# The last two blocks cut as 704 and 256 tokens, the last stores on two queues, the first batch's scaling on two engines, and a new order of all steps

## The chip, the cores and the metric

One core of one Trainium2 chip runs the whole kernel. The metric is the device time of one execution in microseconds (us), the median over several runs. The core's engines are TensorE (PE, with its weight loads listed apart as PEld), VectorE (DVE), ScalarE (ACT), GpSimd (POOL) and SyncE (SP). DMAs are issued from the instruction streams of SP, ACT and POOL.

## The reference

Inputs and output are fp32; q, k and v have 4 batches of 6080 tokens and 256 columns.

```python
qn = q / (np.linalg.norm(q, axis=1, keepdims=True) + 1e-06)   # norms over the 6080 tokens
kn = k / (np.linalg.norm(k, axis=1, keepdims=True) + 1e-06)
s = kn.transpose(0, 2, 1) @ qn / tau                           # 256 x 256 for each batch
a = softmax(s)                                                 # over the last axis
x = (v @ a).reshape(24320, 256)
h = x @ w_in                                                   # 256 -> 2048
out = gelu_tanh(h) @ w_out                                     # 2048 -> 256
```

## The kernel before, in words

**Folding.** For each batch the kernel computes the 256 x 256 matrix of scores and multiplies its exponentials into w_in: `aw` is 256 x 2048, with the softmax's row factors `rs` applied when it is copied out of PSUM. So a token goes from v through `aw`, Gelu and w_out, and v @ a is never formed. All matmuls take bf16 operands and add up in fp32.

**Blocks.** The tokens are cut into 25 blocks, m = 0 to 24, by `SIZES` (L44): five of 1024 and one of 960 in a batch, but in the last batch five of 1024, one of 512 and one of 448. A block is two halves of `hc` tokens (512, 480, and 256 and 224 for the last two), and `hc` is the number of columns that most of its matmuls stream. For each half v is transposed into `vT`: mostly by a cast into a bf16 buffer in DRAM (steps `lv`) and a transposing DMA (`lt`), and for block 0 and the first half of block 1 by PE (`pe_vt`, L341, from what `load_v0` has loaded).

**First layer.** Its 16 chunks of 128 columns of `aw` are done in one of two ways. Plain chunks: steps `jXt` (`mm1_one`, L559) are two matmuls for chunk X and half t, or for both halves at once when t = 2 and the block is narrow; `JXt` (`gelu_one`, L574) is their Gelu on ACT. Pairs of chunks: steps `spm1` to `spm7` (`small`, from L626) take seven matmuls instead of eight for two chunks and both halves, in the manner of Strassen's product, with sums of weights (`sums_w`) and of vT (`sums_v`, steps `vs`); `cq`, `y5`, `ap`, `ax` and the four Gelus `G0, G1, Gr, Gx` (`set_step`) put them together on ACT and DVE.

**Second layer.** Seven products `M1` to `M7` for a block (`product`, L735), each eight matmuls of `hc` columns in two parts A and B, on sums that DVE makes (`T1` to `T4`, `sums_g`). `x1`, `y5`, `y6`, `ap`, `ax`, `a12` combine them, `c11` to `c22` transpose 32 x 32 pieces into the output tile `ot` (pool `yout` with three buffers), and `O0` and `O1` (`store`, L783) write each half with four DMAs of 32 partitions.

**Order.** Nothing is scheduled by a planner at run time. The stretch up to the first `aw` is written out in the code; from there on the text `ORDER` (from L983, 4067 steps) lists every step of all blocks and of batches 1 to 3, and the engines receive their instructions in the order of that list. PSUM's eight banks are handed out by `take` and `give` from a first-in, first-out list (L77), so a new order also changes which step inherits whose bank. The tile framework adds the semaphore waits.

**The head, batch 0.** q and k come in six chunks of rows; for each, ACT and DVE square the elements, PE adds up the squares (`ss_rows`, L213) and the product G of q and k (`gram_first`, L199). The last chunk comes in five pieces (`PIECES`, L137) and is squared by rows (`square_rows`, L174). After it PE transposes v of block 0 (`pe_vt`), `scores` (L359) makes the exponentials on ACT and DVE, DVE and ACT copy one half each of `vT` out of PSUM (L348 to L354), ACT loads the Gelu table (L903), and `first_aw` (L379) computes the sums, the row factors and the first 512 columns of `aw`: DVE scales columns 0 to 255 in four steps (L403), ACT columns 256 to 511 in two (L406). `ORDER` begins with block 0's chunks 0, 1, 2 (`j00`, `j10`, `j20`) and the next part of `aw` (`aw2`, L512, scaled at L525).

**The last stores.** In `store`, the last block's first half to be stored goes to SP, POOL, ACT, POOL, the second alternately to ACT and SP; of the block before it, the third and fourth DMA go to POOL; all others go to SP. A DMA that SP or ACT issues reports to one of eight semaphores, which are used in turn; POOL's DMAs have eight of their own.

Of the kernel before, what the change touches and what calls it, by code (L numbers as in the profile page):

```python
# [18 lines left out]
def kernel(  # L19
# [24 lines left out]
    SIZES = [[1024] * 5 + [960]] * (B - 1) + [[1024] * 5 + [512, 448]]  # L44
# [295 lines left out]

    def pe_vt(m, t):  # L341
        VPS[m, t] = ps = take(("vps", m, t), 1, [128, 2, HALF], f"vt_ps{m}_{t}", BF16)[0]
        for s in range(HALF // 128):
            for cc in range(2):
                nc.tensor.transpose(ps[:, cc, s * 128 : s * 128 + 128],
                                    V0[m, t][:, s, cc * 128 : cc * 128 + 128], ident_bf)

    def pe_vt_copy(m, t, cc):  # L348
        if (m, t, cc) == (0, 0, 1):
            nc.scalar.copy(vt(m)[:, t, cc, :], VPS[m, t][:, cc, :])  # L350
        else:
            nc.vector.tensor_copy(vt(m)[:, t, cc, :], VPS[m, t][:, cc, :])
        if cc == 1:
            give(("vps", m, t))  # L354
# [24 lines left out]
    def first_aw():  # L379
# [21 lines left out]
        for u in range(2):  # L401
            for ic in range(2):
                nc.vector.tensor_scalar_mul(AW[b][:, ic, u * 128 : u * 128 + 128],  # L403
                                            ps[0][ic][:, u * 128 : u * 128 + 128], rs[:, ic : ic + 1])
        for ic in range(2):
            nc.scalar.activation(AW[b][:, ic, 256:512], ps[1][ic], AF.Copy, scale=rs[:, ic : ic + 1])  # L406
# [346 lines left out]
    XS, CS, OT, LAST_OUT = {}, {}, {}, []  # L753
# [28 lines left out]
    def store(m, tj):  # L782
# [13 lines left out]
        if m == LAST:  # L796
            LAST_OUT.append(tj)
# [27 lines left out]
    with tc.manual_schedule():  # L825
# [49 lines left out]
        square_rows(c, 1, 0, 5, "dve")  # L875
# [3 lines left out]
        ss_rows(c, 1, range(0, 5))  # L879
# [19 lines left out]
        pe_vt(0, 0)  # L899
        scores()  # L900
        pe_vt_copy(0, 0, 0)
        pe_vt_copy(0, 0, 1)
        nc.scalar.preload_act_table(AF.Gelu_apprx_tanh)  # L903
# [94 lines left out]
1:s5Gx b1:r3.3 1:s6m3 1:s7y5 0:c21 1:s5m4 1:s6m7 1:M1A 1:s7cq 1:s7m6 1:s5Gr b1:f2.1 1:M1B 1:T3a
1:s6ax 1:s6m4 1:s7m2 b1:r4.0 1:s6G1 b1:r4.1 1:s7ap 1:s7m3 1:T1a 1:s7m7 b1:zq3 1:s6Gx 1:x1 b1:lk6
1:s6Gr b1:lq6 1:s7ax 2:j30 1:s7G0 b1:lq7 b1:r4.2 1:s7G1 2:j11 1:s7m4 2:j01 1:T2a 1:s7Gx 1:s7Gr  # L1000
b1:f3.1 2:j20 2:vs0 2:vs1 1:M2A 2:J30 2:J20 1:T3b 2:s2m1 3:lv1 1:M2B 2:J11 2:s2m5 1:c11 2:s2cq 1:M6A
1:T1b b1:zq5 2:s2m6 1:M5A 2:s2m2 2:s2y5 b1:zq4 2:s2ap 1:T2b 2:s2G0 2:J01 2:j10 b1:dk4 1:M5B 2:vs2
0:c22 2:j21 2:s3m1 2:J10 2:s2m3 1:y5 0:O1 2:J21 3:lt1 2:s2G1 1:M6B 2:s3cq 2:j00 2:J00 1:ap 2:s2m7
# [6 lines left out]
b1:r5.3 2:s6ap 2:s7m5 2:s5Gr 2:s6m7 b1:f5.2 b1:lk7 2:T3a 2:s6ax 2:s7cq 2:s6m3 b1:lk8 2:M1B 2:s7m6  # L1010
3:j30 2:s6m4 2:s7y5 b1:r6.0 2:s7m2 b1:lq8 4:lv1 2:s7ap 2:s7m3 2:s7m7 2:s6G1 2:s6Gx 2:T1a 2:s6Gr
2:s7ax 2:T2a b1:r6.1 b1:r6.2 3:j00 b1:r6.3 3:J30 b1:lq11 b1:lk9 2:s7G0 2:s7G1 3:s2m1 3:J00 2:s7m4
b1:lq9 b1:f6.1 2:M5A 3:j11 2:s7Gx 3:j20 2:T3b 2:s7Gr 2:x1 3:j21 3:vs0 3:J11 b1:zq7 2:M2A b1:lk10
3:J21 3:j01 b1:f5.3 2:M2B 2:T1b 3:J20 3:J01 3:s2m5 3:vs1 5:lv1 3:s2cq b1:r7.0 2:c11 2:M6A b1:r7.1
3:s3m1 3:s2m6 2:M5B 3:s2m2 b1:r7.2 2:T2b 3:s2y5 b1:zk7 b1:r7.3 3:s2ap 3:s2m7 b1:lk11 3:vs2 b1:f5.4
3:s3cq b1:zq8 b1:dk8 3:s2ax 3:s2m3 b1:r8.0 2:y5 3:s2G1 5:lv0 3:s3m2 2:M6B 3:s3m5 3:s2m4 3:s3m6
3:s2G0 3:s3G0 3:j10 3:s3y5 b1:f7.1 3:s2Gr 3:s4m1 3:s2Gx b1:lq10 3:s4cq 2:ap b1:r8.1 2:M3A 3:s3ap
3:J10 3:s3m3 2:T4a 3:s3G1 3:s3m7 2:M3B 3:s4m5 b1:r8.2 3:s4m2 3:s3ax b1:f7.2 3:s5m1 b1:zq9 b1:zk9
2:M7A 3:s3m4 2:M7B 3:s4m6 3:s4G0 2:T4b 3:s4y5 3:s5m5 4:lt0 b1:r8.3 2:c12 3:s5cq 3:s3Gr b1:r9.0
b1:f9.1 b1:f7.3 3:s5m6 3:s6m1 3:s4ap 3:s5y5 2:ax 3:s4m3 3:s3Gx 3:s4G1 3:s4m7 3:s5ap 3:s5m2 3:s5G0  # L1020
2:M4A 3:s6cq 3:s4ax 3:s5m3 b1:r9.1 b1:f7.4 3:s6m5 1:O0 b1:dk10 3:s5m7 3:s4Gx 3:s6y5 3:s4m4 3:s4Gr
3:s6m6 3:s5G1 4:lt1 3:s6m2 2:M4B 3:s7m5 b1:r9.2 3:s5ax 3:s6ap 3:s6m7 3:s7m1 3:s5Gx 2:c21 3:s6m3
3:s5m4 3:s6G0 3:s6ax b1:r9.3 b1:r10.0 2:O0 b1:r10.1 3:s6m4 5:lt0 3:s7y5 3:s7cq b1:f8.1 b1:r10.2
b1:r10.3 3:s6Gx 3:s6Gr b1:r11.0 3:T3a 3:s7m6 b1:r11.1 4:j00 b1:r11.2 3:s5Gr 3:s6G1 3:s7ap 4:s2m1
b1:r11.3 4:J00 3:s7m3 3:s7m7 b1:gc 3:T1a 3:s7ax 3:M1A 3:T2a 4:s2cq 4:j11 4:s2m2 3:s7G1 3:s7m4 4:s3m1
4:vs0 3:s7Gx 4:s2G0 3:s7m2 5:lt1 4:J11 3:T3b 3:M1B 4:vs1 4:s2m5 3:M5A 3:T1b 3:s7Gr 3:x1 3:s7G0 3:M2A
# [288 lines left out]
```

## Time and profile before

| what | value |
|---|---|
| median of 3 runs | 683.74 us (683.71 to 683.79) |
| the profiled execution | 683.82 us |
| its span, first to last instruction | 682.1 us |
| granted PE clock, mean | 0.998 |
| PE busy | 660.3 us, 97%, 3412 matmuls |
| ACT busy | 640.7 us, 94%, 1241 instructions |
| DVE busy | 630.5 us, 92%, 935 instructions |
| POOL busy | 90.1 us, 13% |
| DMA | 78.80 MB, mean 116 GB/s |

Times inside the trace count from the start of the span. A busy share is an average over stages: PE is idle for a good part of the first 50 us, and hardly ever behind them. A line of the trace's timeline has the start and the busy time of a group of instructions, engine, line, operation, the tiles it writes and reads with their shapes, and in brackets the idle time ahead of it with what ended it. In the table of busy time by stretch the columns are the stretch, its length, busy time (and count) of PE, PEld, DVE, ACT and POOL, then the granted PE clock, the DMA engines' share and GB/s.

### The profile page before, as it was taken

To read this page: it belongs to the slowest core of one execution; us is meant where nothing else is said; L and a number is where in the kernel's file an instruction comes from. 1 tells how busy PE (TensorE), PEld (TensorE's weight loads), DVE (VectorE), ACT (ScalarE), POOL (GpSimd) and SP (SyncE) were. 2 spreads that over 40 slices of the span, in tenths; PEclk is the share of its full clock that TensorE was granted. 3 is DMA by queue.
4 is the path that set the end of the run, shared out by engine and by line. 5 is a ranking of instruction groups with operands and counts; after the bars stand their busy time and mean duration, and the time that the engine had idled before them with its cause. 6 is when DMAs were issued, how large, how long until landed. Compare 5 with 4: busy or idle time off the path is not lost.

```text
span 682.1 us, 10254 instructions
## 1 busy us (share of the span) xinstructions
PE 660.3 (97%) x3412; PEld 333.9 (49%) x3472; DVE 630.5 (92%) x935; ACT 640.7 (94%) x1241; POOL 90.1 (13%) x165
## 2 busy tenths in 40 slices
PE   3999999999999999999999999999999999999996
PEld 2844444544445454454444544454444444444465
DVE  3579999999999999999999999999999999999996
ACT  5389999999999999999999999999999999999983
POOL 4323112111100122101020201200000000000002
PEclk9999999999999999999999999999999999999999
DMA  9997868878545896646884477668343446262453
GB/s 241 208 254 134 148 116 140 144 124 147 109 81 105 130 170 112 116 91 116 137 142 78 82 133 137 100 117 132 61 80 62 78 68 118 43 86 46 76 100 60
DMA packets 164678, 78.80 MB, mean 116 GB/s; under 512 B 148545, under 2 KB 153025, under 8 KB 163905
## 3 DMA queue, kind: packets, MB, share of 16 engines
q0 software_dynamic: 18064, 39.84, 32.9%
q1 hardware_dynamic: 145552, 37.09, 30.3%
q10 hardware_dynamic: 1008, 1.22, 0.6%
q8 instruction: 27, 0.44, 0.3%
q14 instruction: 27, 0.21, 0.1%
HBM read 78.91 MB, written 36.57 MB: 169 GB/s over the span
## 4 chain that ended last, share of the span: by engine, by line
PE 79%; ACT 14%; DMA 4%; issue 2%; POOL 0%; DVE 0%; POOLq 0%; DVEq 0%; ACTq 0%
PE u L750 20%; PE rb L639 15%; PE j L571 11%; PE p L750 10%; PE qb L639 7%; PE c L750 5%; PE G L304 4%; DMA qk<-in_k_dram 4%; PE qa L639 3%; ACT qa L654 2%; ACT g L583 2%; PE awp L512 2%; ACT g L664 2%; ACT yw L657 2%; ACT g L673 2%
## 5 line engine op out<-in xcount | busy, mean ns | idle before, releaser
L750 PEld LDWEIGHTS <-wcomb 128*128 128x128 bf16 x1400 | 136.9, 98 | 143.4
L750 PE MATMUL u<-t,wcomb 128*128 128x512 bf16 (+3 forms) x590 | 144.1, 368 | 0.4
L583 ACT ACTIVATE g<-j 128x512 bf16<-128x512 f32 (+1 forms) x196 | 119.0, 664 | 2.0 <-PE j L571 2.0
L571 PE MATMUL j<-vT,aw 128*128 128x512 bf16 (+2 forms) x410 | 114.6, 376 | 1.0 <-ACT aw L406 0.3
L659 DVE TENSOR_TENSOR qb<-rb,yw 128x512 f32<-128x512 f32 (+3 forms) x142 | 95.7, 676 | 9.2 <-PE rb L639 4.1
L639 PE MATMUL rb<-tv,sw 128*128 128x512 bf16 (+3 forms) x276 | 99.8, 372 | 0.4
L662 DVE TENSOR_TENSOR xw<-rb,yw 128x512 f32<-128x512 f32 (+3 forms) x142 | 94.5, 667 | 6.1 <-PE rb L639 3.1
L750 PE MATMUL p<-g,wcomb 128*128 128x512 bf16 (+3 forms) x393 | 96.4, 368 | 0.4
L673 ACT ACTIVATE g<-xw 128x512 bf16<-128x512 f32 (+3 forms) x142 | 94.3, 666 | 0.0
L670 ACT ACTIVATE g<-rb 128x512 bf16<-128x512 f32 (+3 forms) x142 | 88.7, 636 | 2.6 <-PE rb L639 2.5
L654 ACT ACTIVATE qa<-rb 128x512 f32<-128x512 f32 (+3 forms) x142 | 89.3, 633 | 1.4 <-PE rb L639 0.5
L667 ACT ACTIVATE g<-qb 128x512 bf16<-128x512 f32 (+3 forms) x142 | 88.7, 630 | 1.9 <-PE qb L639 1.5
L657 ACT ACTIVATE yw<-qb 128x512 f32<-128x512 f32 (+3 forms) x142 | 89.1, 632 | 1.5 <-PE qb L639 1.0
L664 ACT ACTIVATE g<-qa 128x512 bf16<-128x512 f32 (+3 forms) x142 | 88.7, 631 | 0.3 <-PE qa L639 0.2
L639 PEld LDWEIGHTS <-sw 128*128 128x128 bf16 x568 | 55.3, 98 | 58.2 <-issue 1.2
L571 PEld LDWEIGHTS <-aw 128*128 128x128 bf16 x428 | 41.6, 98 | 44.0 <-issue 1.5
L639 PEld LDWEIGHTS <-aw 128*128 128x128 bf16 x426 | 41.7, 98 | 42.4 <-issue 0.4
L317 POOL DMA_DIRECT2D vb<-in_v_dram x47 | 23.5, 501 | 276.9 <-PE qb L639 123.0
L729 DVE TENSOR_TENSOR t<-g,g 128x2048 bf16<-128x2048 bf16 (+3 forms) x50 | 58.0, 1162 | 0.3
L731 DVE TENSOR_TENSOR t<-g,g 128x2048 bf16<-128x2048 bf16 (+3 forms) x50 | 58.2, 1163 | 0.1
L723 DVE TENSOR_TENSOR g<-g 128x2048 bf16<-128x2048 bf16 (+3 forms) x50 | 58.1, 1162 | 0.2
L733 DVE TENSOR_TENSOR t<-t,g 128x2048 bf16<-128x2048 bf16 (+3 forms) x50 | 57.7, 1160 | 0.0
(133 smaller groups left out, 1002.7 us busy)
## 6 DMA issues: line engine op xcount, KB each, us to landing
out_dram<-ot SPq DMA_DIRECT2D x160, 128.0 KB, 3.0
vb<-in_v_dram POOLq DMA_DIRECT2D x37, 256.0 KB, 5.1
q<-in_q_dram POOLq DMA_DIRECT2D x33, 256.0 KB, 5.4
k<-in_k_dram POOLq DMA_DIRECT2D x33, 256.0 KB, 5.8
out_dram<-ot SPq DMA_DIRECT2D x24, 120.0 KB, 2.7
wst<-in_moe_w_out_dram POOLq DMA_DIRECT2D x2, 1024.0 KB, 11.2
qk<-in_q_dram POOLq DMA_DIRECT2D x3, 512.0 KB, 14.3
qk<-in_k_dram POOLq DMA_DIRECT2D x3, 512.0 KB, 17.0
```

Source lines behind the costliest of these rows:

```text
L571: GATE[0] = nc.tensor.matmul(hp[:, :n].rearrange("p (t x) -> p t x", t=2) if t == 2 else hp[:, :n], lhsT=AW[b][:, cc, fc * 128 : fc * 128 ...
L583: nc.scalar.activation(g[:, t, fc % 8, :hc], hp[:, :hc], AF.Gelu_apprx_tanh)
L639: GATE[0] = nc.tensor.matmul(acc[:, :hc], lhsT=lhs, rhs=rhs, start=i in (1, 5), stop=True, skip_group_check=True)
L654: nc.scalar.activation(Q0[m, p][:, :hc], RB[m, p][:, :hc], AF.Copy)
L657: nc.scalar.activation(YW[m, p][:, :hc], Q1[m, p][:, :hc], AF.Copy)
L659: nc.vector.tensor_add(Q1[m, p][:, :hc], RB[m, p][:, :hc], YW[m, p][:, :hc])
L662: nc.vector.tensor_add(XW[m, p][:, :hc], RB[m, p][:, :hc], YW.pop((m, p))[:, :hc])
L664: nc.scalar.activation(g[:, 0, e, :hc], Q0.pop((m, p))[:, :hc], AF.Gelu_apprx_tanh)
L667: nc.scalar.activation(g[:, 1, e, :hc], Q1.pop((m, p))[:, :hc], AF.Gelu_apprx_tanh)
L670: nc.scalar.activation(g[:, 0, e + 1, :hc], RB.pop((m, p))[:, :hc], AF.Gelu_apprx_tanh)
L673: nc.scalar.activation(g[:, 1, e + 1, :hc], XW.pop((m, p))[:, :hc], AF.Gelu_apprx_tanh)
L750: GATE[0] = nc.tensor.matmul(ACCS[m, acc][:, :hc], lhsT=wcomb[:, w, fc, :], rhs=x[:, fc, :], start=first and k_ == 0, stop=k_ == 3, skip_g ...
```

## The change

1. `SIZES`: the last two blocks are of 704 and 256 tokens (`hc` 352 and 128) instead of 512 and 448 (256 and 224).
2. In the head's last chunk DVE squares three rows of k instead of five and ACT the other two; DVE adds rows 2 and 3 onto rows 0 and 1, and PE adds up three rows instead of five.
3. v of block 0's first half is transposed into two PSUM tiles, one for each half of the columns, and DVE copies both (before: one tile, one copy on DVE, one on ACT).
4. `first_aw` scales in four pieces of 128 columns and two rows each. ACT takes one row's part of the first two pieces, DVE the six others. The Gelu table is loaded behind ACT's two, instead of ahead of `first_aw`.
5. `store`: the last block's eight stores alternate between ACT and SP; POOL has none of them.
6. `ORDER` is new, with 4061 steps. Its first 125 steps are those of before. Block 23 goes from 6 plain chunks and 5 pairs to 4 plain chunks (each half by itself) and 6 pairs, block 24 from 12 plain chunks and 2 pairs to 16 plain chunks; all other blocks keep their division, and the steps stand in another order in most stretches.

```diff
-    SIZES = [[1024] * 5 + [960]] * (B - 1) + [[1024] * 5 + [512, 448]]
+    SIZES = [[1024] * 5 + [960]] * (B - 1) + [[1024, 1024, 1024, 1024, 1024, 704, 256]]
...
+    def fold_pair(c):
+        o = SQ0[c][:, 0:2, 256:512]
+        nc.vector.tensor_add(o, o, SQ0[c][:, 2:4, 256:512])
...
+    def pe_vt_first():
+        for cc in range(2):
+            VPS[0, 0, cc] = ps = take(("vps", 0, 0, cc), 1, [128, HALF], f"vt_ps0_0{cc}", BF16)[0]
+            for s in range(HALF // 128):
+                nc.tensor.transpose(ps[:, s * 128 : s * 128 + 128], V0[0, 0][:, s, cc * 128 : cc * 128 + 128], ident_bf)
+
+    def pe_vt_first_copy():
+        for cc in range(2):
+            nc.vector.tensor_copy(vt(0)[:, 0, cc, :], VPS[0, 0, cc])
+            give(("vps", 0, 0, cc))
...
-        for u in range(2):
+        for u in range(4):
             for ic in range(2):
-                nc.vector.tensor_scalar_mul(AW[b][:, ic, u * 128 : u * 128 + 128],
-                                            ps[0][ic][:, u * 128 : u * 128 + 128], rs[:, ic : ic + 1])
-        for ic in range(2):
-            nc.scalar.activation(AW[b][:, ic, 256:512], ps[1][ic], AF.Copy, scale=rs[:, ic : ic + 1])
+                o, x = AW[b][:, ic, u * 128 : u * 128 + 128], ps[u // 2][ic][:, u % 2 * 128 : u % 2 * 128 + 128]
+                if u < 2 and ic:
+                    nc.scalar.activation(o, x, AF.Copy, scale=rs[:, ic : ic + 1])
+                else:
+                    nc.vector.tensor_scalar_mul(o, x, rs[:, ic : ic + 1])
+            if u == 1:
+                nc.scalar.preload_act_table(AF.Gelu_apprx_tanh)
...
-            if m == LAST and not LAST_OUT:
-                eng = (nc.sync, nc.gpsimd, nc.scalar, nc.gpsimd)[bi]
-            elif m == LAST:
+            if m == LAST:
                 eng = (nc.scalar, nc.sync)[bi % 2]
...
-        square_rows(c, 1, 0, 5, "dve")
+        square_rows(c, 1, 0, 3, "dve")
+        square_rows(c, 1, 3, 5, "act")
+        fold_pair(c)
...
-        ss_rows(c, 1, range(0, 5))
+        ss_rows(c, 1, (0, 1, 4))
...
-        pe_vt(0, 0)
+        pe_vt_first()
         scores()
-        pe_vt_copy(0, 0, 0)
-        pe_vt_copy(0, 0, 1)
-        nc.scalar.preload_act_table(AF.Gelu_apprx_tanh)
+        pe_vt_first_copy()
         first_aw()
```

The end of the list, before and after:

```text
(before)
...
23:M3A 24:T3a 23:M3B 24:s6cq 24:s7m7 23:M7A 24:s7ax 24:s6m6 24:s6y5 21:O0 24:s7m3 23:c12 23:M7B
24:s7G1 24:s7m4 24:s6ap 23:ax 24:s7Gx 24:j52 23:c22 24:J52 24:j62 24:s7Gr 24:s6m3 24:s6G1 23:M4A
24:T1a 24:s6m7 24:s6ax 24:J62 23:M2A 24:M5A 24:s6Gx 23:M4B 24:M1A 24:s6m4 24:T2a 22:O1 24:s6m2
24:T3b 22:O0 24:M1B 23:M2B 24:s6Gr 24:T1b 24:x1 23:O1 24:s6G0 24:T2b 24:M5B 24:T4a 24:M6A 23:c21
24:y5 24:T4b 24:M6B 24:M3A 24:M3B 24:y6 24:M7A 23:c11 24:a12 24:M7B 23:O0 24:M2A 24:M2B 24:ax 24:c12
24:M4A 24:M4B 24:c22 24:O1 24:c11 24:c21 24:O0

(after)
...
23:x1 22:M4B 23:M6A 24:J62 23:T3b 23:T1b 23:M5B 23:s7Gr 23:s4Gr 23:T2b 24:ja2 23:y5 23:M6B 24:Ja2
22:c21 24:j12 24:jb2 23:ap 24:Jb2 24:j72 22:c22 24:J12 23:s6m4 24:j92 23:M7A 24:J72 23:M7B 23:M3A
24:J92 23:T4a 24:j52 23:M3B 23:s6Gr 23:ax 24:j02 24:j32 22:O0 23:c22 23:c12 24:je2 24:J02 24:J32
24:j22 24:j82 24:J52 24:J22 24:J82 24:jf2 24:jc2 24:Jf2 23:T4b 22:O1 23:M4A 24:Je2 24:j42 24:Jc2
24:jd2 24:M1A 24:T3a 23:M2A 24:J42 24:Jd2 24:T1a 24:T2a 24:M1B 24:M5A 24:T3b 24:T1b 24:x1 23:M4B
24:T2b 24:M6A 24:M5B 24:M6B 23:c21 24:T4b 24:y5 23:M2B 24:y6 24:M3A 24:M7A 24:T4a 24:M7B 23:c11
24:ax 24:M3B 24:a12 24:M2A 23:O1 24:M2B 24:c22 24:M4A 23:O0 24:c12 24:M4B 24:c21 24:O1 24:c11 24:O0
```

More of the change, by code (lines that the diff above doesn't have):

```diff
@@ L348, in pe_vt_copy @@
     def pe_vt_copy(m, t, cc):
[L349 to L352, printed above, removed]
+        nc.vector.tensor_copy(vt(m)[:, t, cc, :], VPS[m, t][:, cc, :])
         if cc == 1:
@@ L998 @@
[L998 to L1003, printed above, removed]
@@ L1010 @@
[L1010 to L1015, printed above, removed]
@@ L1016 @@
[L1016 to L1026, printed above, removed]
-4:s3cq 4:s2y5 4:s2m6 3:M2B 4:s3m5 b1:zq11 4:s2ap b1:zq10 6:lv1 3:T2b 3:M5B 7:lv0 b1:f9.2 4:s3y5
@@ new lines @@
+11:J01 b2:aw2 b2:ac3 b2:aw1 b2:aw4 10:s7G1 13:lt0 10:s7ax b2:ac1 10:s7Gx b2:aw0 b2:aw7 10:T1a
+10:s6Gr 9:O0 b2:ac7 10:M1A 10:T3b 9:c22 10:s7m4 b2:ac2 11:j11 b2:aw5 b2:aw6 10:M1B 12:lt1 11:vs0
+10:T1b 11:s2m1 10:s7Gr b2:ac4 11:vs1 b2:ac0 10:T2a 10:x1 11:vs2 10:M5A b2:ac6 10:T2b 11:J11 11:j30
+10:M2A 11:J30 10:M2B 11:j00 11:s2cq b2:ac5 11:s2m5 10:c11 9:O1 11:s2m6 11:s2m2 11:s3m5 12:lt0
+11:s2y5 11:s2G0 10:M5B 11:s3y5 11:s2ap 11:s3m1 11:J00 11:s2m7 11:s2m3 b2:w00 11:s2ax 10:M6A 11:s2m4
+11:s3cq 11:s2G1 11:s3m6 10:y5 11:s2Gr 11:s3m2 10:T4a 11:s3G0 11:s3ap 11:s4m1 10:M6B 11:j20 16:lv0
@@ new lines @@
+23:j01 23:s2ap 23:J11 23:s2m3 23:s2G1 23:J01 23:s3ap 23:s2m7 22:M5A 23:s3m3 23:s3G1 23:s3m7 23:s5m1
+23:s5m5 22:T1b 23:s2ax 22:M6A 23:s5cq 23:s2m4 23:s3ax 23:s5y5 22:T2b 23:s3m4 23:s5m6 22:M5B 23:s5m2
+23:s2Gr 23:s4m1 23:s3Gr 23:s5ap 23:s5m3 22:c11 22:T4a 22:y5 22:M6B 23:s4cq 23:s5G1 23:s5G0 22:ap
+23:s4m2 23:s4m5 23:s4G0 23:s5m7 23:s4y5 23:s5ax 23:s7m5 23:s4m6 23:j00 23:s4ap 21:O0 23:s7y5 23:s7m1
+22:M3A 23:s4m7 22:T4b 23:J00 23:s7cq 23:s5m4 22:M3B 23:s5Gx 23:s5Gr 23:s4ax 23:s7m2 22:c12 23:s4m3
```

550 lines of the change are left out of this document (280 added, 270 removed).

## The prediction

> **What bounds the kernel now.** I read the page first (busy times and slices), then busy time by stretch, then the timeline of the two ends.
>
> ```profile
> span 682.1 us, 10254 instructions
> PE 660.3 (97%) x3412; PEld 333.9 (49%) x3472; DVE 630.5 (92%) x935; ACT 640.7 (94%) x1241; POOL 90.1 (13%) x165
> PE   3999999999999999999999999999999999999996
> PE 79%; ACT 14%; DMA 4%; issue 2%; POOL 0%; DVE 0%; POOLq 0%; DVEq 0%; ACTq 0%
> ```
>
> ```profile
> 37.00:50.00 13.00, 11.95 (x66) 5.61 (x67) 10.50 (x24) 10.94 (x21) 2.02 (x4) 1.00 1.16 275
> 50.00:676.00 626.00, 622.70 (x3107) 308.52 (x3163) 601.76 (x881) 612.83 (x1204) 70.72 (x130) 1.00 0.61 106
> ```
>
> The first slice and the last are the only thin ones for TensorE (PE). Between 50 and 676 us PE is busy 622.70 of 626.00 us at a granted clock of 1.00. So the middle is bound by the columns that PE streams: no new order of the same columns can win more than these 3.3 us there, and any wait that it opens is paid in full. Time can be won before 50 us, after PE's last matmul, or by fewer columns. The profiled execution took 683.82 us (span 682.1 and 1.7 around it), 0.08 above the median 683.74; I work out differences on its trace and subtract them from the median.
>
> What PE pays for a column, by the chain in order of time (first fence) and the timeline (second):
>
> ```profile
> 57.63 0.86 PE u L750 x4
> ```
>
> ```profile
> 35.31 0.61 PE L345 MATMUL vt_ps<-ident_bf,v 128*128 128x128 bf16 x8
> 672.02 0.93 PE L750 MATMUL u<-t,wcomb 128*128 128x224 bf16 x8
> ```
>
> Four matmuls of 512 columns take 0.86 us: 0.215 us each, 0.42 ns a column. At 224 columns (0.93 less the last one's 0.26, over seven steps) it is 0.096 us, 0.43 ns a column. At 128 columns, with fresh weights for each, 0.61 less 0.22 over seven steps gives 0.056 us, 0.43 ns. Narrow matmuls stay proportional.
>
> **Part 1, the head: scaling and table load.** Timeline of the stretch in which the first scaled weights appear:
>
> ```profile
> 36.41 0.58 ACT L350 COPY vT<-vt_ps 128x512 bf16<-128x512 bf16 x1
> 36.66 0.17 DVE L397 RECIPROCAL rs<-sums 128x2 f32<-128x2 f32 x1 [0.28 <-PE sums L394]
> 36.94 1.13 DVE L403 TENSOR_SCALAR aw<-aw_ps,rs 128x128 bf16<-128x128 f32 x4
> 37.02 1.28 ACT L903 ACT_TABLE_LOAD   x1
> 38.31 0.84 ACT L406 ACTIVATE aw<-aw_ps,rs 128x256 bf16<-128x256 f32 x2
> 38.84 0.10 PEld L571 LDWEIGHTS <-aw 128*128 128x128 bf16 x1 [0.63 <-ACT aw L406]
> 38.84 0.76 PE L571 MATMUL j<-vT,aw 128*128 128x512 bf16 x2 [0.33 <-ACT aw L406]
> 39.04 1.19 ACT L583 ACTIVATE g<-j 128x512 bf16<-128x512 f32 x2
> 39.43 1.03 PE L512 MATMUL awp<-win_bf,eT 128*128 128x512 bf16 x4
> 40.07 3.38 DVE L525 TENSOR_SCALAR aw<-awp,rs 128x512 bf16<-128x512 f32 x5 [2.00 <-PE awp L512]
> 40.93 1.09 ACT L583 ACTIVATE g<-j 128x512 bf16<-128x512 f32 x2 [0.70 <-PE j L571]
> ```
>
> Now: the factors are there at 36.83. DVE scales columns 0 to 255 in four steps about 0.26 apart. ScalarE (ACT) copies vT, loads the Gelu table until 38.30, and only then scales columns 256 to 511. So the third first-layer matmul pair (j20) has its weights at 38.84 and 39.2, and the aw matmuls behind it on PE start at 39.43. DVE has been idle for 2.00 us when they feed it at 40.07.
>
> After: DVE does both vT copies. The transposes that feed them end at 35.92, DVE is free from its two products with G at about 35.6, and two copies with steps of 0.33 end at about 36.5, before the reciprocal at 36.66: free. ACT scales two pieces of 128 columns from about 36.93 (0.47 for one of 256 by the row at 38.31, so some 0.36 each) until 37.6, beside DVE, then loads the table until about 38.9. DVE scales six pieces, 36.94 to 38.6; those that j20 needs are its third and fourth, done at 37.8 and 38.06. PE: j00 from 37.35, then four matmuls at 0.215 (j00's second, j10, j20's first), each with its weights ready by then: j20 ends at about 38.7 instead of 39.43. **Gain 0.75 us** (0.6 to 0.85). The first Gelu starts at 38.9 instead of 39.04, so the later table load costs nothing; ACT then waits for PE as before (the 0.70 at 40.93).
>
> That shift must reach 50 us. DVE's run of five scalings starts when PE feeds it, so it moves too. What could hold it is a load that lands at a fixed time:
>
> ```profile
> v<-in_v_dram POOLq DMA_DIRECT2D x1, 256.0 KB, 10.1
> ```
>
> ```profile
> 46.87 0.61 PE L345 MATMUL vt_ps<-ident_bf,v 128*128 128x128 bf16 x8
> ```
>
> The v tile issued at 35.74 lands at 45.84; PE transposes it at 46.87, which would become 46.1: 0.3 us of cover left. If it were gone, the difference would be lost to PE directly. I take the whole 0.75.
>
> The Trainium skill (ScalarE: Activation LUTs, What ACT_TABLE_LOAD costs) counts a drain of 1.38 us on top of a table load of 1.28; then the first Gelu of the new order would come at 40.3, and some 0.6 of this gain would be gone. The trace shows 1.28 and the next ACTIVATE 0.01 us behind it, and the trace decides.
>
> **Part 2, the last piece of the squares.** DVE squares three k rows instead of five, ACT two, and DVE adds rows 2 and 3 onto 0 and 1, so PE sums three rows instead of five.
>
> ```profile
> 30.14 1.06 ACT L180 ACTIVATE sq<-qk 128x1024 bf16<-128x1024 bf16 x1 [2.85 <-DMA qk<-in_q_dram]
> 31.62 1.99 DVE L182 TENSOR_TENSOR sq<-qk 128x1280 bf16<-128x1280 bf16 x3 [0.83 <-DMA qk<-in_k_dram]
> 32.71 1.03 PE L231 MATMUL ss<-sq,ones_bf 128*128 128x256 bf16 x8
> 33.89 0.42 DVE L182 TENSOR_TENSOR sq<-qk 128x512 bf16<-128x512 bf16 x1 [0.29 <-DMA qk<-in_q_dram]
> ```
>
> Two matmuls of 256 columns fewer are 0.22 us. But the add waits for ACT's square (31.62 plus about 0.65), runs 0.42 until 32.75 and delays the next DVE square by some 0.15; PE's three sums start at 32.8, the next three wait for that square until 33.3 and end at 33.6, where the eight ended before. And the last q rows still wait for their DMA at 33.89. I take **0** (from 0.15 gained to 0.1 lost).
>
> **Part 3, columns.** Counting the steps of the list: blocks 23 and 24 stream 29,440 and 26,432 columns before (55,872), 40,128 and 15,360 after (55,488); all other blocks are the same. 384 fewer at 0.42 ns: **gain 0.16 us**. ACT and DVE work on the same number of steps within a few and on 1 to 4% more columns in these two blocks; they hide under PE (601.76 and 612.83 of 626 above, and successive steps overlap).
>
> **Part 4, the end.** Timeline, stores by window, and the closing instructions:
>
> ```profile
> 675.08 0.93 PE L750 MATMUL u<-t,wcomb 128*128 128x224 bf16 x8
> 675.55 1.82 ACTq L795 DMA_DIRECT2D out_dram<-ot  x3
> 676.05 0.42 DVE L779 STREAM_TRANSPOSE ot<-u 128x224 f32<-128x224 f32 x1 [0.23 <-PE u L750]
> ```
>
> ```profile
> out_dram<-ot SPq DMA_DIRECT2D x2, 56.0 KB, 2.7
> out_dram<-ot ACTq DMA_DIRECT2D x2, 56.0 KB, 3.0
> ```
>
> ```profile
> out_dram<-ot SPq DMA_DIRECT2D x1, 56.0 KB, 1.9
> out_dram<-ot ACTq DMA_DIRECT2D x1, 56.0 KB, 2.0
> ```
>
> ```profile
> L1310 POOLq DRAIN  x3: 46/102/5016, 676.3 to 681.8; - x3
> L1310 SPq DRAIN  x3: 7/7/7, 680.9 to 681.5; - x3
> ```
>
> PE streams until e = 675.08 + 8 x 0.096 = 675.85. The final transpose starts 0.20 later, the last stores are issued at 676.5 to 677.4 and take 2.7 to 3.0 us (1.9 to 2.0 for the pair a microsecond earlier). SP has seen all of them at 680.9, e + 5.05. POOL, which issued four late stores, drains from 676.25 for 5.02 us, until 681.27, 0.35 behind SP; closing takes 0.85 more.
>
> After: block 24's O1 rows are ready at about e + 0.1, and ACT issues two stores at once, SP two, 0.4 apart. Then comes **a wait that the change adds**: the eight landing semaphores of the hardware queues go round, and in the new listing SP's two stores of O0 wait for those that ACT's two O1 stores have just taken. Behind them on SP is only the end. So: e + 0.5 (ACT's second), landing 2.2 (above 2.0, because block 23's O0 stores, 352 tokens, were issued 1 us earlier), then SP's last store, landing 1.9 without a crowd: e + 4.6, plus 0.4 for SP's row of waits, e + 5.0 against 5.05. POOL's last store is now block 23's, about 1 us before e, so its drain should end ahead of SP: 0.35 saved. **Gain 0.40 us**, from 1.1 (both landings 1.7) to a loss of 1.2 (3.0 and 2.7). The shorter final transpose (0.3 for 128 columns, by 0.42 for 224) helps nothing behind that wait.
>
> **Part 5, the new order.** In the middle both lists have the same columns. I take 0, between 0.4 gained (of the 3.3) and 1.5 lost.
>
> **Sum**: 0.75 + 0 + 0.16 + 0.40 + 0 = 1.31 us; 683.74 - 1.31 = 682.4.
>
> **The rivals.**
> 1. *New order opens gaps.* A matmul that starts a bank waits for the instruction that frees it. Of the last 45 hand-overs the old list has one with a single step between, the new list four, all in block 23 (s4m1 behind s2Gr, s7cq behind J00, M5A behind G1, x1 behind G0). Each may cost PE about 0.25 us: 1.0 in all, 683.4. Against it: similar hand-overs at two to five steps left PE at 99.5%.
> 2. *The two landings in series take long.* With 3.0 and 2.7 SP is done at e + 6.6, 1.2 later than now: 684.0, slower. It decides from a sum of 5.4 us for both. For it: those rows. Against: they stand for eight stores of 56 KB at once, and now they have 32 KB.
> 3. *Weights bind the narrow block.* Block 24's 56 products have 128 columns. If a weight load of 0.098 us could not overlap the next, they would cost 56 x 0.044 = 2.5 us more: 684.9, slower; this overtakes the gain from 0.078 us a matmul.
>
> ```profile
> L750 PEld LDWEIGHTS <-wcomb 128*128 128x128 bf16 x1400 | 136.9, 98 | 143.4
> ```
>
> Against it stand the 0.056 of the transposes. The Trainium skill (TensorE: Matmul & The Clock Gate, Back-to-back issue gap) gives about 81 ns for pairs of load and matmul at 128 columns; by that rule 56 x 0.025 = 1.4 us would be added and the time would be 683.8. The row at 35.31, with a load for each matmul, speaks against it.
> 4. *More is won.* Landings of 1.7 (1.1 instead of 0.40) and 0.1 of the middle: 681.6.
> 5. *The head does not move*, because something else holds PE until 39.4 or the v tile comes late: 683.2.
>
> **How the numbers follow.** Forecast 0.44 (own range 681.9 to 683.0), rival 1 0.20, 2 0.09, 3 0.04, 4 0.19, 5 0.04. The bound of 0.2% is 1.37 us, about what a measurement of this kernel tells from no change; the forecast lies 0.06 inside it. Faster: half the forecast and rival 4, 0.41. Slower than 685.1: 0.03 each of rivals 2 and 3 where they run longer than their sums, and 0.02 of rival 1 where its gaps pass 2.7 us: 0.08; same 0.51. The range 681.5 to 683.8 leaves out rivals 2 and 3, the long part of 1 and a sliver of 4, under 0.2.
>
> **What would show it.** Right: j20 ends near 38.7 and the aw matmuls start there; the last squares unchanged at 33.9 and S at 34.8; block 24's products about 0.055 apart; SP's last two stores issued 2 us after its others; POOL's drain ends before SP's. Wrong: gaps above 0.2 us between PE's matmuls in block 23, SP done later than e + 5.4, or a head that has lost its 0.75 by 50 us.

## The result, and the profile after

The changed kernel takes **682.43 us** (median of 19 runs, 682.23 to 682.77), the kernel before 683.71 us (median of 19 runs of the same series): ratio 0.9981, 95% interval 0.9974 to 0.9988. That is 1.28 us or 0.19% less, where 1.31 was forecast; the interval leaves out that nothing changed. The profiled execution took 682.53 us.

The page of the kernel after, its first lines and the chain's shares:

```profile
span 680.7 us, 10235 instructions
...
PE 659.0 (97%) x3415; PEld 332.1 (49%) x3475; DVE 631.3 (93%) x934; ACT 639.9 (94%) x1241; POOL 89.4 (13%) x163
...
PE   3999999999999999999999999999999999999996
...
PE 88%; DMA 4%; ACT 4%; DVE 1%; issue 1%; POOL 0%; SPq 0%; DVEq 0%; ACTq 0%; POOLq 0%
```

Nothing of its shape has changed: PE is full but for the first slice and the last. ACT's share of the chain has fallen from 14% to 4%. To see where 1.28 us went, the same matmuls have to be found in both traces. Both lists hold the same steps up to certain points, so PE has the same work behind it there. The row to follow is `awp` (the matmuls of `aw` of batches 2 and 3), in the chain of waits in order of time (start, length); first the kernel before, then after:

```profile
331.03 2.16 PE awp L512 x10
496.22 1.73 PE awp L512 x8
```

```profile
330.20 2.16 PE awp L527 x10
494.72 1.73 PE awp L527 x8
```

And the head, in the timeline of the kernel after:

```profile
36.42 0.17 DVE L409 RECIPROCAL rs<-sums 128x2 f32<-128x2 f32 x1 [0.17 <-PE sums L406]
36.68 0.63 ACT L417 ACTIVATE aw<-aw_ps,rs 128x128 bf16<-128x128 f32 x2 [0.56 <-PE aw_ps L401]
36.70 1.64 DVE L419 TENSOR_SCALAR aw<-aw_ps,rs 128x128 bf16<-128x128 f32 x6
37.33 1.28 ACT L421 ACT_TABLE_LOAD   x1
37.34 1.24 PE L586 MATMUL j<-vT,aw 128*128 128x512 bf16 x5 [0.28 <-DVE aw L419]
38.42 1.03 PE L527 MATMUL awp<-win_bf,eT 128*128 128x512 bf16 x4
38.62 1.09 ACT L598 ACTIVATE g<-j 128x512 bf16<-128x512 f32 x2
```

Batch 0's `awp` starts at 38.42, not 39.43: 1.01 us earlier. At 330 us the lead is 0.83, at 495 us 1.50. Two rows of the timeline of the end follow: SP's last two stores, and PE's last product:

```profile
677.73 0.79 SPq L808 DMA_DIRECT2D out_dram<-ot  x2
```

```profile
673.76 0.61 PE L765 MATMUL u<-t,wcomb 128*128 128x128 bf16 x8
```

It streams until e = 673.76 + 8 x 0.056 = 674.21, where the kernel before had 675.85: a lead of 1.64. But the span is only 1.39 shorter (682.05 and 680.67 in the two traces), so 0.25 has gone again behind PE's last matmul. With that the forecast's terms can be read off. The head with the squares: 1.01 (forecast 0.75), of which 0.19 is a load that landed earlier and 0.05 the squares (below). The middle: 0.49 (forecast 0); 0.30 of it is a stall at 382 us that goes with the changed head and not with the order (experiments four and six). Blocks 23 and 24 with their fewer columns: 0.14 (forecast 0.16). The end: minus 0.25 (forecast plus 0.40). These terms add up to the 1.39 between the two traces, or 1.20 without the landing; the medians differ by 1.28. The total was right because two errors of opposite sign cancel, and that is luck.

### The profile page after: what moved, and what is told of

The parts are those of the page before. It is cut to its first block, busy times and chain, and to the rows that moved or that the text cites. A ratio compares the mean times of both kernels' runs of the same rounds, so it can differ in the third digit from the quotient of the medians.

```text
span 680.7 us, 10235 instructions
## 1 busy us (share of the span) xinstructions
PE 659.0 (97%) x3415; PEld 332.1 (49%) x3475; DVE 631.3 (93%) x934; ACT 639.9 (94%) x1241; POOL 89.4 (13%) x163
## 4 chain that ended last, share of the span: by engine, by line
PE 88%; DMA 4%; ACT 4%; DVE 1%; issue 1%; POOL 0%; SPq 0%; DVEq 0%; ACTq 0%; POOLq 0%
PE u L765 23%; PE rb L654 17%; PE j L586 12%; PE p L765 11%; PE qb L654 8%; PE c L765 5%; PE G L308 4%; DMA qk<-in_k_dram 4%; PE qa L654 4%; PE awp L527 2%; ACT g L598 1%; ACT qa L669 1%; ACT g L682 0%; ACT yw L672 0%; ACT sq L278 0%
## 5 line engine op out<-in xcount | busy, mean ns | idle before, releaser
L598 ACT ACTIVATE g<-j 128x512 bf16<-128x512 f32 (+2 forms) x204 | 123.2, 657 | 1.6 <-PE j L586 1.5
L586 PE MATMUL j<-vT,aw 128*128 128x512 bf16 (+3 forms) x425 | 114.8, 367 | 0.7 <-DVE aw L419 0.3
L674 DVE TENSOR_TENSOR qb<-rb,yw 128x512 f32<-128x512 f32 (+2 forms) x141 | 95.9, 682 | 7.2 <-ACT yw L672 3.0
L677 DVE TENSOR_TENSOR xw<-rb,yw 128x512 f32<-128x512 f32 (+2 forms) x141 | 94.6, 672 | 6.7 <-PE rb L654 4.5
L654 PE MATMUL rb<-tv,sw 128*128 128x512 bf16 (+2 forms) x275 | 100.3, 374 | 0.4
L688 ACT ACTIVATE g<-xw 128x512 bf16<-128x512 f32 (+2 forms) x141 | 94.5, 673 | 0.4 <-DVE xw L677 0.3
L672 ACT ACTIVATE yw<-qb 128x512 f32<-128x512 f32 (+2 forms) x141 | 89.2, 639 | 1.4 <-PE qb L654 0.9
L669 ACT ACTIVATE qa<-rb 128x512 f32<-128x512 f32 (+2 forms) x141 | 89.8, 641 | 0.8 <-PE rb L654 0.2
L685 ACT ACTIVATE g<-rb 128x512 bf16<-128x512 f32 (+2 forms) x141 | 88.5, 639 | 0.3
L679 ACT ACTIVATE g<-qa 128x512 bf16<-128x512 f32 (+2 forms) x141 | 88.6, 637 | 0.2
```

What stands on the lines that cost most here:

```text
L586: GATE[0] = nc.tensor.matmul(hp[:, :n].rearrange("p (t x) -> p t x", t=2) if t == 2 else hp[:, :n], lhsT=AW[b][:, cc, fc * 128 : fc * 128 ...
L598: nc.scalar.activation(g[:, t, fc % 8, :hc], hp[:, :hc], AF.Gelu_apprx_tanh)
L654: GATE[0] = nc.tensor.matmul(acc[:, :hc], lhsT=lhs, rhs=rhs, start=i in (1, 5), stop=True, skip_group_check=True)
L669: nc.scalar.activation(Q0[m, p][:, :hc], RB[m, p][:, :hc], AF.Copy)
L672: nc.scalar.activation(YW[m, p][:, :hc], Q1[m, p][:, :hc], AF.Copy)
L674: nc.vector.tensor_add(Q1[m, p][:, :hc], RB[m, p][:, :hc], YW[m, p][:, :hc])
```

## The experiments

Theory A takes the traces at their word: scaling 0.77, squares 0.05, columns 0.16, order 0.49, end minus 0.25. The main rivals are those of the forecast: the order is worth nothing, and the end gains. Each experiment is compared with runs of the kernel before on the same chip (683.49 to 683.79 us in the five series). Two of these series, on one chip and with nothing changed, gave 683.76 and 683.49, and the 95% intervals below reach 0.5 to 0.9 us to each side. So a difference under about half a microsecond is carried by the traces and not by the runs alone.

**One: the scaling alone** (parts 3 and 4 of the change in the kernel before).

```diff
-        pe_vt_copy(0, 0, 0)
-        pe_vt_copy(0, 0, 1)
-        nc.scalar.preload_act_table(AF.Gelu_apprx_tanh)
+        pe_vt_first_copy()
         first_aw()
...
-        for u in range(2):
+        for u in range(4):
```

> The kernel before with parts 3 and 4 of the change alone: both vT copies on DVE, the scaling of aw shared in pieces of 128 columns, the table load behind ACT's two. Theory A (the traces: PE is 0.77 us earlier behind this stretch, beyond the 0.24 it had won before it, and keeps it to the end): 0.77 us faster than before, 682.95. Rival (what is won in the head is lost again at a load that lands at its own time): within 0.15 of before, 683.6.

Measured 683.07 against 683.77 (ratio 0.9988, 0.9979 to 0.9997): 0.70 us. From the reciprocal to `awp` its trace has 2.00 us (36.60 to 38.60) where the kernel before has 2.77 (36.66 to 39.43). Theory A holds, the gain survives past 50 us.

**Two: the table load alone.**

```diff
-        nc.scalar.preload_act_table(AF.Gelu_apprx_tanh)
         first_aw()
...
             nc.scalar.activation(AW[b][:, ic, 256:512], ps[1][ic], AF.Copy, scale=rs[:, ic : ic + 1])
+        nc.scalar.preload_act_table(AF.Gelu_apprx_tanh)
```

> The kernel before with the Gelu table's load moved behind ACT's two scalings of 256 columns, and nothing else of the change. Theory A (the table load ahead of ACT's scalings is the whole loss in the head, sharing the scaling out in pieces adds nothing): ACT's scalings end at 37.9 instead of 39.2, the third first-layer pair ends at 38.6, 0.70 us gained as with the whole of parts 3 and 4: 683.05. Rival (the pieces and the copies on DVE are needed, since ACT still copies vT first): 0.3 gained, 683.45.

Measured 683.17 against 683.76 (0.9991, 0.9982 to 1.0000): 0.59 us, with an interval that just reaches no change. The timeline:

```profile
36.38 0.17 DVE L397 RECIPROCAL rs<-sums 128x2 f32<-128x2 f32 x1 [0.28 <-PE sums L394]
...
36.95 0.84 ACT L406 ACTIVATE aw<-aw_ps,rs 128x256 bf16<-128x256 f32 x2 [0.22 <-PE aw_ps L389]
37.32 1.34 PE L572 MATMUL j<-vT,aw 128*128 128x512 bf16 x5 [0.31 <-DVE aw L403]
37.80 1.28 ACT L407 ACT_TABLE_LOAD   x1
38.50 1.03 PE L513 MATMUL awp<-win_bf,eT 128*128 128x512 bf16 x4
39.10 0.60 ACT L584 ACTIVATE g<-j 128x512 bf16<-128x512 f32 x1
```

From the reciprocal to `awp` it takes 2.12 us. So the place of one table load is 0.65 of the 0.77; the pieces of 128 columns and the second copy on DVE add 0.12, which theory A had put at nothing. In the traces of the kernel after, of experiment one and of this one the Gelu starts 0.01 or 0.02 us behind the end of the load. The Trainium skill (ScalarE: Activation LUTs, What ACT_TABLE_LOAD costs) counts a drain of 1.38 us on top of the load; no run here shows it.

**Three: the squares alone.**

```diff
-        square_rows(c, 1, 0, 5, "dve")
+        square_rows(c, 1, 0, 3, "dve")
+        square_rows(c, 1, 3, 5, "act")
+        fold_pair(c)
...
-        ss_rows(c, 1, range(0, 5))
+        ss_rows(c, 1, (0, 1, 4))
```

> The kernel before with part 2 of the change alone: five k rows of the last piece squared by DVE and ACT, two rows folded, three sums on PE instead of five. Theory A (the traces: PE is 0.24 us earlier behind the last squares): 683.47. Rival (the prediction: the last q rows wait for their DMA, which lands when it lands; the 0.2 between the traces is a landing that came earlier by chance): 683.7.

Measured 683.36 against 683.77 (0.9993, 0.9984 to 1.0002): 0.41 us, more than either said, but the interval holds no change as well. The trace does not have it at the squares. From the square of the k rows of the chunk before to the scores (`S`) the kernel before takes 6.06 us (first fence), this one 6.02 (second):

```profile
28.77 1.23 DVE L172 TENSOR_TENSOR sq<-qk 128x2048 bf16<-128x2048 bf16 x1 [3.31 <-DMA qk<-in_k_dram]
34.83 0.76 DVE L373 TENSOR_TENSOR S<-G,rk 128x256 f32<-128x256 f32 x2 [0.51 <-PE ss L225]
```

```profile
28.44 1.23 DVE L172 TENSOR_TENSOR sq<-qk 128x2048 bf16<-128x2048 bf16 x1 [3.00 <-DMA qk<-in_k_dram]
...
32.42 0.96 PE L235 MATMUL ss<-sq,ones_bf 128*128 128x256 bf16 x6
...
34.46 0.76 DVE L377 TENSOR_TENSOR S<-G,rk 128x256 f32<-128x256 f32 x2 [0.47 <-PE ss L229]
```

The whole of this stretch starts when a DMA lands, and that comes at 28.43 to 28.82 us in the profiles of this study: one profile alone can't tell 0.2 us in the head. In this run's profile it comes 0.33 earlier than in that of before; when it came in the other executions of either kernel is not on record, so the landing stays a rival for the 0.41. Two more runs take the stretch apart.

Only the squaring shared, without the fold (five sums on PE as before):

> The kernel before with DVE squaring three of the five k rows and ACT two, without the fold: PE still adds up five rows. Tells which half of part 2 gave its 0.41 us in the runs. Theory A (the last q rows' landing binds, as the trace has it, and the 0.41 are landings that come at another time in another build): between 683.4 and 683.8 with no pattern. Rival B (PE's two sums fewer are the gain): 683.75. Rival C (the earlier squares are the gain): 683.4.

Measured 683.74 against 683.76 (0.9999, 0.9990 to 1.0008): nothing. Rival C falls; theory A and rival B both said this.

Two matmuls of 256 columns that nothing uses, behind the five sums:

> The kernel before with two more matmuls of 256 columns behind PE's five sums of the last k rows, 0.22 us of PE that nothing uses. Theory A (PE waits for the last q rows behind them, 0.29 us of cover): no change, 683.75. Rival B (PE's sums bind the head in most runs, so that two fewer gained and two more lose): 684.0 or more.

Measured 683.82 against 683.76 (1.0003, 0.9994 to 1.0011). The runs show no loss, as theory A said, and rival B's 684.0 did not come. But in the trace:

```profile
28.56 1.23 DVE L172 TENSOR_TENSOR sq<-qk 128x2048 bf16<-128x2048 bf16 x1 [3.05 <-DMA qk<-in_k_dram]
...
34.82 0.76 DVE L373 TENSOR_TENSOR S<-G,rk 128x256 f32<-128x256 f32 x2 [0.73 <-PE ss L225]
```

That is 6.26 us, 0.20 more than before: in this stretch the two matmuls are paid in full. So by the trace PE has no cover there, against theory A and against the forecast; that 0.20 is lost over the whole kernel the runs neither show nor exclude. In the kernel before PE in fact never stops:

```profile
33.58 0.60 PE L206 MATMUL G<-qk 128*128 128x256 bf16 x4
34.02 0.24 PE L225 MATMUL ss<-ones_bf,sq 128*128 128x1 bf16 x4
34.12 0.60 PE L206 MATMUL G<-qk 128*128 128x256 bf16 x4
34.55 0.24 PE L225 MATMUL ss<-ones_bf,sq 128*128 128x1 bf16 x4
```

DVE's 0.29 us of waiting for the last q rows is wait on an engine that nobody is waiting for. What keeps the two sums that part 2 saves (0.22) down to about 0.05 is that its last three sums wait for DVE's square behind the fold: the six take 0.96 us, where the eight of before took 1.03 and six in a row would take 0.82.

**Four: the squares undone in the changed kernel.**

```diff
-        square_rows(c, 1, 0, 3, "dve")
-        square_rows(c, 1, 3, 5, "act")
-        fold_pair(c)
+        square_rows(c, 1, 0, 5, "dve")
...
-        ss_rows(c, 1, (0, 1, 4))
+        ss_rows(c, 1, range(0, 5))
```

> The changed kernel with part 2 undone: DVE squares all five k rows, PE adds up five. The other side of the run with part 2 alone, which was 0.41 us faster than before where its trace shows 0.04 at the squares and a stall of 0.30 at 382 us that is not there. Theory A (the squares themselves give 0.04, and the changed kernel has no stall at 382 us to lose): 0.05 slower than the changed kernel, 1.2 faster than before. Rival (part 2 gives 0.4 in every surrounding): 0.4 slower than the changed kernel, 0.87 faster than before.

Measured 683.26 against 683.79 (0.9993, 0.9984 to 1.0002): 0.53 faster than before, which is 0.75 short of the changed kernel's 1.28. The interval reaches from 1.09 faster to 0.14 slower: theory A's 1.2 lies outside it and falls, the rival's 0.87 lies inside. The chain's `awp` rows show that this run is 0.27 behind the changed kernel by 330 us, of which 0.15 is the landing, and that by 495 us it is 0.56:

```profile
330.47 2.16 PE awp L523 x10
495.28 1.73 PE awp L523 x8
```

PE's weight loads show where the rest is: two stalls that the changed kernel has not, for which the profile names no releaser ("issue"). They cost PE 0.29 and 0.25 us.

```profile
415.36 0.10 PEld L582 LDWEIGHTS <-aw 128*128 128x128 bf16 x1 [0.39 <-issue]
512.06 0.10 PEld L650 LDWEIGHTS <-sw 128*128 128x128 bf16 x1 [0.36 <-issue]
```

The kernel before has one of the same kind at 382 us, which costs PE 0.30 us. Nothing else moves then but one packet of a queue of instructions (the second fence: its DMA queues from 381.7 to 382.4 us):

```profile
382.21 0.10 PEld L639 LDWEIGHTS <-aw 128*128 128x128 bf16 x1 [0.41 <-issue]
```

```profile
q14 instruction: 1, 0.01, 4.1%
```

But it is not PE that was late. By its semaphore the matmul at 382.21 waits for DVE's `qb`, which runs from 381.46 to 382.16. DVE could have started it 0.40 us sooner, since the ACT `g` that its bracket names had ended at 381.06 (timeline of the kernel before):

```profile
380.40 0.66 ACT L664 ACTIVATE g<-qa 128x512 bf16<-128x512 f32 x1
381.46 0.70 DVE L659 TENSOR_TENSOR qb<-rb,yw 128x512 f32<-128x512 f32 x1 [0.71 <-ACT g L664]
```

In the run of part 2 alone DVE has two instructions more ahead of this point, the fold and a semaphore wait. There the late one is `xw`, ahead of `qb`, and no matmul of PE is held up by that:

```profile
380.08 0.69 DVE L666 TENSOR_TENSOR xw<-rb,yw 128x512 f32<-128x512 f32 x1 [0.22 <-issue]
380.82 0.70 DVE L663 TENSOR_TENSOR qb<-rb,yw 128x512 f32<-128x512 f32 x1
```

Counted in the traces with their semaphore waits, both are DVE's 704th instruction, and 704 is 5 x 128 + 64. Each of the ten stalls of this kind in the profiles of this study has such a late instruction, of DVE or of ACT, at number 64 behind a multiple of 128. The queue fits that count. In the trace of before q14 brings 26 packets of 8192 bytes, and ACT, DVE, SP and POOL together have 3354 instructions there: 64 bytes for each, 128 in a packet (an estimate from these numbers). So the stall goes with the instructions of the engine that PE waits for. What that engine does in these 0.2 to 0.4 us, the profiles don't show. The stall would be 0.30 of the 0.41 of part 2 alone.

**Five: a shorter instruction stream of PE, by itself.**

```diff
-        warm(6)
+        warm(4)
         pe_vt(0, 0)
```

> The kernel before with two idle matmuls fewer in the stretch in which PE waits for the scores (four instead of six, 34.7 to 35.3 us), so that PE's instruction stream is as much shorter as with part 2 of the change, and nothing else is touched. Theory F (0.30 us of what part 2 gives in the runs is a stall at 381.7 us in which PE's sequencer waits for a packet of its own instructions, and a stream that is shorter by two matmuls gets the packet earlier): the stall is gone, 0.3 us faster than before, 683.45. Rival (part 2's gain in the runs comes from the squares or is chance): the stall stays, 683.75.

Measured 683.48 against 683.49 (1.0001, 0.9992 to 1.0010). The stall stays:

```profile
382.04 0.10 PEld L639 LDWEIGHTS <-aw 128*128 128x128 bf16 x1 [0.41 <-issue]
```

Theory F falls. It took the stall for a wait for PE's own instructions; two matmuls fewer on PE leave DVE's 704th instruction where it was, on `qb`. Stalls of this kind, of 0.2 to 0.3 us, stand in the profiles of eight of the fourteen kernels of this study, at 382, 415, 448, 512 or 653 us, and in none of those of the changed kernel, of part 2 alone and of experiment six. Where they fall goes with the number of instructions that DVE or ACT has run: the two runs of experiment three that have no fold keep the one at 382 us, part 2 alone has it not. That is read off fourteen traces without an exception; no experiment changed this number by itself. That the stalls account for most of what part 2 does in the runs is read off the traces too.

**Six: the old order of the middle, in the changed kernel.** In this diff and in those of seven and ten `before[a:b]` and `after[a:b]` stand for steps a + 1 to b of the two lists; each kernel holds the steps written out.

```diff
-ORDER = after[0:4061]
+ORDER = after[0:125] + before[125:3500] + after[3500:4061]
```

> The changed kernel with the steps 126 to 3500 of its list put back in the order of before; the head, the last 561 steps, the block sizes and the stores stay changed. Theory A (the traces: from 59.8 to 588 us PE gains another 0.49 us with the new order, by stalls of the old order at 382 and 442 to 453 us that are gone): 0.49 slower than the changed kernel, 682.9. Rival (the prediction: the order in the middle is worth nothing): 682.4.

Measured 683.01 against 683.77 (0.9990, 0.9981 to 0.9999): 0.76 faster than before, so 0.52 slower than the changed kernel. Theory A holds in its size. Its `awp` rows:

```profile
330.52 2.16 PE awp L527 x10
495.43 1.73 PE awp L527 x8
```

It loses 0.39 us to the changed kernel between these two rows. Matmul by matmul, three waits of 0.12 to 0.18 us at 442, 452 and 453 us stand in every kernel with the old order, and in none with the new; in the trace of before they make 0.40. The stall at 382 us does not come back: it goes with the head's number of instructions. So the old order costs 0.46 between the first `awp` (38.67 here, 38.42 in the changed kernel) and the one at 495 us. The traces of before and after, less the stall, give 0.19 for the same thing: 0.40 for the three waits, less 0.22 that the new order loses at 289 us. The two do not agree, so the worth of the order is known only to lie near 0.2 to 0.5.

**Seven: the new tail alone** (block sizes, last 561 steps, stores) in the kernel before. The edit of the stores is part 5 of the change, which this diff leaves out.

```diff
-ORDER = before[0:4067]
+ORDER = before[0:3500] + after[3500:4061]
...
-    SIZES = [[1024] * 5 + [960]] * (B - 1) + [[1024] * 5 + [512, 448]]
+    SIZES = [[1024] * 5 + [960]] * (B - 1) + [[1024, 1024, 1024, 1024, 1024, 704, 256]]
```

> The kernel before with the new block sizes, the new last 561 steps and the new queues of the last stores; the head and the first 3500 steps are those of before. Theory A (the traces: 0.16 us fewer columns, but the end from PE's last matmul to the last instruction is 0.25 longer, since SP's last two stores wait 3 us for ACT's): 0.1 slower than before, 683.8. Rival (the prediction: 0.16 and 0.40 gained): 683.15.

Measured 684.17 against 683.77 (1.0005, 0.9996 to 1.0014): 0.40 slower, with an interval that holds theory A's 0.1 and no change; the rival's gain of 0.56 lies outside it. Its trace has one more stall of 0.18 at 653 us, behind DVE's 1216th instruction (9 x 128 + 64), which the changed kernel has not.

**Eight: the ring of semaphores (t1).** In the kernel after SP's queue waits once for a store (its waits from 670 us on), and the closing drains end so:

```profile
SPq L808 <- DMA out_dram<-ot: 2.5, 1, 2.5
```

```profile
L1320 POOLq DRAIN  x3: 46/93/5354, 673.9 to 680.4; - x3
L1320 SPq DRAIN  x3: 7/7/7, 679.8 to 680.1; - x3
```

The first DMA of ACT was issued at 674.36 and SP goes on at 677.69. The trace has the semaphore's number with each store. ACT's two stores of O1 report to 116 and 117 and land at 677.67 and 677.90; SP's last two, issued at 677.73 and 678.10, take 116 and 117 again. The eight numbers that SP and ACT share are used again and again, but not strictly in turn. The stores by window, from 674 to 675 us and from 678 to 679:

```profile
out_dram<-ot ACTq DMA_DIRECT2D x2, 32.0 KB, 3.2
```

```profile
out_dram<-ot SPq DMA_DIRECT2D x2, 32.0 KB, 1.5
```

The edit puts all four stores of O1 on SP, so that the semaphores that SP's last two stores take are those of block 23's stores:

```diff
             if m == LAST:
-                eng = (nc.scalar, nc.sync)[bi % 2]
+                eng = nc.sync if tj else (nc.scalar, nc.sync)[bi % 2]
```

> The changed kernel with all four last stores of O1 on SP (two of them were on ACT); O0 stays on ACT and SP in turn. SP's last two stores then find semaphores that block 23's stores held, not those of ACT's stores of a moment before. Theory A (the wait for ACT's landing, 674.7 to 677.7 us, is what makes the end long): SP is done near 679.0, GpSimd's drain at 679.25 becomes the last, 0.6 us gained on the changed kernel: 681.85. Rival (the DMA engines are busy with block 23's stores until 677.5 anyway, and the last landings come when they come): 682.4.

Measured 681.82 against 683.76 (0.9972, 0.9961 to 0.9983): 1.94 faster than before, 0.66 more than the changed kernel. In its trace 116 and 117 were last held by two of block 23's stores, which landed at 675.28 and 676.08, and SP issues its last two at 676.50 and 676.91 without a wait. Theory A holds, and the drain of GpSimd is now the last:

```profile
L1320 POOLq DRAIN  x3: 46/93/5305, 674.1 to 679.9; - x3
L1320 SPq DRAIN  x3: 7/7/7, 679.0 to 679.6; - x3
```

SP's first drain starts at 679.0; GpSimd's long one starts at 674.08 and takes 5.30, until 679.38.

**Nine: without GpSimd at the end (t5)**, on top of the edit of eight.

```diff
             elif m == LAST - 1 and bi > 1:
-                eng = nc.gpsimd
+                eng = nc.gpsimd if tj else nc.scalar
```

> The changed kernel with the stores of the t1 run, and block 23's last two stores (of O0) on ACT instead of GpSimd. Theory A (in the t1 run GpSimd's drain, which ends 5 us after its last store, is the last by 0.33 us): the drain ends near 674 and SP's last landing near 678.9 sets the end, 0.35 us faster than the t1 run, 681.45. Rival (two more stores on ACT's queue ahead of its own two make the last landing later by as much): 681.8.

Measured 681.57 against 683.49 (0.9971, 0.9960 to 0.9983): 1.92 faster than before, no more than the run ahead of it. The time itself is near theory A's 681.45, but the kernel before is 0.27 lower in this series too. In its trace SP is done at 679.1, where GpSimd's drain ended at 679.4; the difference is too small for these runs. The rival's 'no gain' came, by another way than it said: the last landing is not later (678.52, in eight 678.85). SP's closing waits for the semaphores come one behind the other, 0.06 to 0.07 us each, and nine of them stand behind the one for this landing, where in eight it was nearly the last.

**Ten: with a stretch of the old order**, on top of nine. By the traces the new order loses 0.22 us at 289 us, between steps 1501 and 1750.

```diff
-ORDER = after[0:4061]
+ORDER = after[0:1501] + before[1501:1750] + after[1750:4061]
```

> The t5 run with steps 1502 to 1750 of the list in the order of before. Theory A (by the traces the new order loses 0.22 us in that stretch, a stall at 289 us that the old order does not have): 0.2 us faster than the t5 run, 681.25. Rival (what the new order loses there it has gained by 390 us): 681.45.

Measured 681.25 against 683.49 (0.9967, 0.9955 to 0.9980): 2.24 faster than before and 0.32 faster than the run ahead of it on the same chip. In its trace the stall at 289 us is gone; the trace gives 0.22 for that, and the rest is within what runs can't tell. This version beats both kernels.

## Why the prediction was right, and where it was not

The forecast was 682.4, the range 681.5 to 683.8; 682.43 came. By its own steps:

1. **The head, 0.75: right.** 0.77 in the trace, 0.70 in the run of its own. The two pieces on ACT took 0.63 us together, not 0.72, and the whole stretch began 0.24 earlier, so the table load ended at 38.61, not 38.9. The reason given, ACT's table load ahead of its scalings, is 0.65 of it (experiment two). The v tile's cover held: no part of the gain was lost by 60 us.
2. **The squares, 0: right in size, wrong in its reason.** 0.05 came. "The last q rows still wait for their DMA" names a wait of DVE; PE, on which all hangs, works through and had no cover in the trace (6.26 for 6.06 us with two more matmuls). The other half of the reason, the sums that wait behind the fold, is what holds the gain down. The runs show more than the stretch does, 0.41 and 0.75 us, and the traces put most of that on stalls far behind it, which come and go with the number of DVE's and ACT's instructions (experiment four); for the 0.41 the landing is a rival.
3. **Columns, 0.16: right**, 0.14 from 495 us to e. The products of 128 columns took 0.056 us each, so the third rival did not come, nor did gaps in block 23 (rival 1): no wait of PE over 0.06 us stands behind 300 us in the trace after.
4. **The end, plus 0.40: wrong, it lost 0.25.** The wait was where the prediction put it, with SP's last two stores behind ACT's landings. The term that was mis-sized is that landing: 2.2 us assumed, 3.3 measured for the first of the two. The DMA engines had block 23's O0 stores, 352 KB that were issued from 673.2 us on, and 128 KB of O1 itself, and were busy from 674.1 to 677.3:

```profile
DMA  0000000009979797989878720000342500000000
```

   (share of the DMA engines in 40 slices from 672 to 681.2 us.) "Issued 1 us earlier" was taken for a reason that the landings would be nearly free; it should have been a reason to add up the bytes. That the landings were slow for that reason is read off this row, not shown by an experiment. So SP was done at e + 5.6 and not e + 5.0, past the e + 5.4 that the prediction itself named as a sign of being wrong. This is rival 2's mechanism at 3.3 and 1.5 where it decides from 5.4 for both; it stayed on the near side, and experiment eight shows that the wait cost 0.66.
5. **The new order, 0: wrong, it gained 0.2 to 0.5.** 0.4 was the upper bound given. The three waits at 442 to 453 us that it removes (0.40) were in the trace of before, inside the 3.3 us of PE's idle time that the prediction took as a bound and didn't take apart; experiment six shows their worth. The stall at 382 us (0.30), the rest of the 0.49 in the middle, was in that trace too; it went with the number of instructions in the head, which no term of the forecast had.

So a gain in the middle that was not forecast and the mechanism of rival 2 came together, and the sum landed on the forecast by luck, on a path that differs from it in two of five terms.

## What to carry to other kernels

Where stores share a few semaphores, look up in the trace which store last held the one that each of the last stores takes: a store that takes the semaphore of one issued a moment ago waits for its whole landing, and moving two DMAs to another queue gave back 0.66 us. Ahead of a table load, ask who needs the engine next: moving one load of 1.28 us behind two short scalings was 0.59 of the 0.70 us won there in the runs, 0.65 of 0.77 in the traces. And before a wait is called cover, look whether the engine that waits is the one on the path; a DVE that waits for a load says nothing of PE.

## What the runs showed of the hardware that was not expected

PE stalls for 0.2 to 0.3 us although every engine that it depends on seems free. It waits for an instruction of DVE or ACT that began 0.2 to 0.4 us later than the trace gives a reason for. In all ten cases this is number 64 behind a multiple of 128 of that engine's instructions, and the packets of the instruction queue, 8192 bytes each, hold 128 by the estimate above. So an instruction or two more in the head move the stall to another step, where it may cost nothing: it is at 382 us in the kernel before, at 448 in the run of the scaling alone, at 415 and 512 in the changed kernel with the old squares. A change of 0.05 us in the head came out as 0.41 us in one surrounding and 0.75 in another; each of these is uncertain by more than half a microsecond, and by the traces the greater part of it came that way. And GpSimd's closing drain takes 5.0 to 5.4 us in the kernel before, after and in experiment eight, and 6.2 and 6.6 in nine and ten; in all of them it ends 1.9 to 2.1 us behind the landing of GpSimd's last store. So a store on GpSimd less than some 5 us ahead of the end can set it.
